# Zero regions of two cache gradients: two stored from GpSimd as two-row stores, the last one in steps of rows

## The chip, the cores and the metric

The kernel runs on one core of one Trainium2 chip. The metric is the device time in microseconds (us) of one execution; less is better. Three executions of the kernel before took 282.73, 282.97 and 284.07 us, median 282.97.

The core has five engines that run side by side and wait for each other by semaphores: PE (TensorE, matrix products and transposes), DVE (VectorE), ACT (ScalarE), POOL (GpSimd) and SP (SyncE, which here only issues DMAs). Sixteen DMA engines move data between HBM and the on-chip memory.

## The reference

One decode step of a transformer block and its gradients. With `xn` the layer-normed input, the forward part is

```
q  = xn @ wq                                # 4 batches, 32 heads of 128
k, v = k_cache[:, :, Sk-W:], v_cache[...]   # last W = 1024 of Sk = 4096 positions, 8 kv heads
p  = softmax(q k^T / sqrt(128));  o = p v
out = x + o @ wo + (gelu(xn @ w_gate) * (xn @ w_up)) @ w_down
_out, _vjp = jax.vjp(_f, A_x, A_k_cache, A_v_cache, A_wq, A_wo, B_w_gate, B_w_up, B_w_down)
_grads = _vjp(grad_out)
```

The outputs are `out` and the gradients of all eight arguments, in bf16. The gradients of `k_cache` (out_2) and `v_cache` (out_3) have the full shape (4, 8, 4096, 128). The forward part uses only the last 1024 positions, so positions 0 to 3071 of both gradients are zero, and these zeros have to be written: 2 tensors x 32 (batch, head) pairs x 3072 x 128 x 2 bytes = 50.3 MB of the 81.0 MB that the page counts as written to HBM.

## The kernel before, in words

**Stages.** First the FFN with its gradients (weights `wg`, `wu`, `wd`), then attention in four groups of two kv heads (`NT` = 4, `GP` = 2), `t` from 0 to 3. For each group the kernel transposes K and V on PE and computes scores (`kv_steps`), softmax and its gradient, `odq` (o and dq) and `fin`, and prepares four kinds of gradient pieces: `dvdk(t, 0)` for dv, `dvdk(t, 1)` for dk, and those of `dw(t)` for wo and wq. A piece is one or two matmuls into a PSUM tile, one eviction by ACT or DVE into a staging tile, and, when the staging tile is full, one store issued by SP.

**Order of the work.** Pieces are put into a queue `bg` and run one at a time by `tick` between the steps of the main work, so the last pieces of a group (dk, wo, wq) run during the next group. The program order on every engine is the order of the Python text (a manual schedule). After the last group `tick(len(bg))` at L754 empties `bg`; `zero(len(zlist))` at L755 issues the zero stores that are left. The short end (L757 to L787) computes out_0 and out_1, whose 4-row stores are issued by ACT.

**Staging tiles.** The pool `stage` has three buffers for `stg_dv` and `stg_dk`, `outp` has four for `osb_o`, `osb_q` and others. An eviction into a buffer waits until the store that used it before has landed.

**Zeros.** `ztile` (128 x 6144 bf16) holds zeros. `zlist` holds 32 zero regions; each covers two heads of one batch of one tensor, 2 x 3072 x 128 elements, and `zero(n)` (L161) stores the next n of them, one DMA of 1536 KB each, with 64 rows of 12288 bytes for each head. Calls of `zero` are spread over the program; here matter the one after each `stg_dv` and `stg_dk` store (L490, in `piece` of `dvdk`), `zero(4)` in the last group (L734) and L755. The second head's dk store of group t (`k` = 1, `g` = 1) is issued in group t + 1; the zero stores after it are issued at 120.75, 168.55 and 210.35 us for t = 0, 1, 2.

**Queues.** SP issues its DMAs in program order. Its DMAs and those of ACT take eight completion semaphores in turn, so a DMA also waits until the eighth DMA before it has landed. GpSimd issues the loads of `wo` and `wq` for the later groups (`load_w`); in the last group it has only the two `o_s` products of L463 left after its last `qmr`.

**Lines used below.** L97 and L98: evictions by ACT and DVE (`evac`). L103: the DMA in `store`, the line under which all stores appear. L279: transposes. L454 to L465: the end of `odq` for k = 0. L484: the dv and dk matmuls. L813: the end of the program.

Of the kernel before, what the change touches and what calls it, by code (L numbers as in the profile page):

```python
# [14 lines left out]
P = 128  # L15
# [3 lines left out]
def kernel(  # L19
# [28 lines left out]
    nc = tc.nc  # L48

    B, Sq, D = A_x.shape  # L50
    _, G, Sk, Dh = A_k_cache.shape
# [4 lines left out]
    K0 = Sk - W  # L56
# [4 lines left out]
    NT = G // GP  # L61
# [38 lines left out]
    def store(eng, out, in_, kind):  # L100

        eng.nop()
        d = eng.dma_start(out=out, in_=in_)  # L103
        for k in ("rest", "zeros") if kind == "rest" else ("rest",):
            tc.declare_no_dep(d.ins, group=k, reason="stores write disjoint parts of the outputs")
        tc.add_to_no_dep_group(kind, d.ins)
        return d
# [12 lines left out]
    def load_w(t, eng=nc.gpsimd):  # L120
        pool = w_pool[t % 2]
        wo_t[t] = pool.tile([P, HG, D], BF16, name="wo_sb", tag="wo")
        eng.dma_start(out=wo_t[t][:], in_=wo_v[t])
        wq_t[t] = pool.tile([P, ND, CW], BF16, name="wq_sb", tag="wq")
        eng.dma_start(out=wq_t[t][:], in_=wq_v[t])
# [30 lines left out]
    ZR = 2  # L156
    ZW = K0 * Dh * ZR // P
    ztile = const.tile([P, ZW], BF16, name="ztile")
    zlist = deque((og, b, g) for b in range(B) for g in range(0, G, ZR) for og in (out_2, out_3))

    def zero(n=1):  # L161
        for _ in range(min(n, len(zlist))):
            og, b, g = zlist.popleft()
            store(nc.sync, og[b, g:g + ZR, 0:K0, :].rearrange("g (m j) d -> m g (j d)", m=P // ZR), ztile[:], "zeros")


    nc.gpsimd.memset(ztile[:], 0.0)
# [276 lines left out]
    def odq(t, k):  # L444
        pT, blks = st[t][("PT", "dST")[k]], (v_t, k_t)[k]
        cols = pT[:].rearrange("p j (y s) -> p j s y", s=SL)
        for j in range(JB):
            q, jj = j // JQ, j % JQ
            for g in range(GP):
                nc.tensor.matmul(od_ps[g * 32:g * 32 + B * rep, k, g, :], lhsT=cols[:, jj, g * NQ + q, :],  # L450
                                 rhs=blks[(t, g)][:, j, :], start=(j == 0), stop=(j == JB - 1),
                                 tile_position=(0, g * 32))
        rows = attw.tile([P, GP, Dh], BF16, name="od_r", tag=f"od_r{k}", bufs=2)
        if k == 0:  # L454
            nc.vector.tensor_copy(out=rows[:], in_=od_ps[:, k])  # L455
        else:
            nc.scalar.activation(out=rows[:], in_=od_ps[:, k], func=ACT.Copy, scale=scale)
        st[t][("o", "dq")[k]] = rows
        if k == 0:

            o_s = attw.tile([P, GP, rep, Dh], BF16, name="o_s", tag="o_s", bufs=2)
            for g in range(GP):
                nc.gpsimd.tensor_tensor(out=o_s[:, g], in0=rows[:, g].unsqueeze(1).broadcast_to([P, rep, Dh]),  # L463
                                        in1=msk_r[:].unsqueeze(2).broadcast_to([P, rep, Dh]), op=ALU.mult)
            st[t]["os"] = o_s  # L465

    def odT(t, k):
        rows = st[t][("o", "dq")[k]]
        T_ps = transposes([rows[:, g, :] for g in range(GP)], "odT")
        rT = attw.tile([P, GP, B, rep], BF16, name="od_T", tag=f"od_T{k}")  # L470
        for g in range(GP):
            nc.vector.tensor_copy(out=rT[:, g].rearrange("p b r -> p (b r)"), in_=T_ps[:, g, g * 32:g * 32 + B * rep])
        st[t][("oT", "dqT")[k]] = rT

    def dvdk(t, k):
        src, mr, og = st[t][("P", "dS")[k]], st[t][("do", "q")[k]], (out_3, out_2)[k]
        nm = ("dv", "dk")[k]

        def piece(g, j, held):
            if j == 0:  # L480
                held["stg"] = stage.tile([P, JB, Dh], BF16, name="stg_" + nm, tag="stg")
            stg = held["stg"]
            mps = ps_w.tile([P, NQ, Dh], FP32, name="kv_ps", tag="w")
            nc.tensor.matmul(mps[:].rearrange("p q d -> p (q d)"), lhsT=src[:, j * P:(j + 1) * P],  # L484
                             rhs=mr[:, g].rearrange("p q d -> p (q d)"), start=True, stop=True)
            evac(stg[:].rearrange("p (q j) d -> p j q d", q=NQ)[:, j], mps[:], 512)
            if j == JQ - 1:
                store(nc.sync, og[:, t * GP + g, K0:Sk, :].rearrange("b (m j) d -> m b (j d)", j=JB),
                      stg[:].rearrange("p j d -> p (j d)"), "rest")
                zero()  # L490

        made = []
        for g in range(GP):
            held = {}
            made.append([lambda g=g, j=j, held=held: piece(g, j, held) for j in range(JQ)])
        return made
# [183 lines left out]
    for f4 in range(NF4):  # L680
        held = {}
        n = min(4, NF - 4 * f4)
# [34 lines left out]
    with tc.tile_pool(name="kv_b", bufs=GP, reuse_waits="tile") as kv_b, \  # L717
            tc.tile_pool(name="w_b", bufs=1, reuse_waits="tile") as w_b, \
            tc.tile_pool(name="stage", bufs=3, reuse_waits="tile") as stage:
        kv_pool[1], w_pool[1] = kv_b, w_b  # L720
        zero()
        pre(0)
        load_w(1)
        load_kv(1, 0)
        for t in range(NT):
            kv_steps(t, 0, 0)
            if t == 0:
                zero()
                load_kv(1, 1)
                zero()  # L730
            softmax(t)
            kv_steps(t, 1, 1)
            if t == NT - 1:
                zero(4)  # L734
            link(len(chain))
            softmax_d(t)
            link()
            odq(t, 0)
            load_kv(t + 2, 1)
            if t + 1 < NT:  # L740
                pre(t + 1)
            link(len(chain))
            odT(t, 0)
            odq(t, 1)
            load_kv(t + 2, 0)
            tick(2)
            odT(t, 1)
            fin(t)
            if t + 2 < NT:
                load_w(t + 2)  # L750
            (k0, k1), (o0, o1, q0, q1) = dvdk(t, 1), dw(t)
            for p in (k0, o0, k1, o1, q0, q1):
                bg.extend(p)
        tick(len(bg))  # L754
        zero(len(zlist))  # L755

        fin_ps = []  # L757
        for o in range(2):
            f_ps = ps_w.tile([B, ND, P], FP32, name="f_ps", tag="w")
            for c in range(ND):  # L760
                nc.tensor.transpose(f_ps[:, c, :], acc[:, o, c, :], ident_f[:])
            fin_ps.append(f_ps)
        acc_o = fin_ps[0][:].rearrange("b c p -> b (c p)")
        acc_d = attw.tile([B, P, ND], FP32, name="acc_d", tag="P_s")
        nc.vector.tensor_copy(out=acc_d[:].rearrange("b p c -> b c p"), in_=fin_ps[1][:])
        acc_d = acc_d[:].rearrange("b p c -> b (p c)")
        out_b = attw.tile([B, D], BF16, name="out_b", tag="pT")
        nc.vector.tensor_tensor(out=out_b[:], in0=acc_o, in1=x4[:], op=ALU.add)
        nc.scalar.dma_start(out=out_0.rearrange("b s d -> (b s) d"), in_=out_b[:])

        s1 = attw.tile([B, 1], FP32, name="s1", tag="m")
        nc.vector.reduce_sum(out=s1[:], in_=acc_d, axis=AX.X)
        pr = attw.tile([B, D], FP32, name="pr", tag="dS_s")
        s2 = attw.tile([B, 1], FP32, name="s2", tag="es")
        nc.vector.tensor_tensor_reduce(out=pr[:], in0=acc_d, in1=xn_f[:], scale=1.0, scalar=0.0,
                                       op0=ALU.mult, op1=ALU.add, accum_out=s2[:])
        nm1 = attw.tile([B, 1], FP32, name="nm1", tag="rr")
        nc.vector.tensor_scalar(out=nm1[:], in0=s1[:], scalar1=-1.0 / D, scalar2=None, op0=ALU.mult)
        nm2 = attw.tile([B, 1], FP32, name="nm2", tag="gs")
        nc.vector.tensor_scalar(out=nm2[:], in0=s2[:], scalar1=-1.0 / D, scalar2=None, op0=ALU.mult)  # L780
        nc.vector.scalar_tensor_tensor(out=pr[:], in0=xn_f[:], scalar=nm2[:, 0:1], in1=acc_d,
                                       op0=ALU.mult, op1=ALU.add)
        nc.vector.tensor_scalar(out=pr[:], in0=pr[:], scalar1=nm1[:, 0:1], scalar2=rstd[:, 0:1],
                                op0=ALU.add, op1=ALU.mult)
        dx_b = attw.tile([B, D], BF16, name="dx_b", tag="E_f")
        nc.vector.tensor_tensor(out=dx_b[:], in0=pr[:], in1=dy4[:], op=ALU.add)
        nc.scalar.dma_start(out=out_1.rearrange("b s d -> (b s) d"), in_=dx_b[:])  # L787
# [30 lines left out]
```

## Time and profile before

| what | value |
|---|---|
| median of 3 executions | 282.97 us |
| the profiled execution's own time | 283.0 us |
| its span, first to last instruction | 281.0 us |
| PE / DVE / ACT / POOL busy | 72% / 58% / 42% / 14% of the span |
| moved by DMA | 112.12 MB, mean 399 GB/s |
| share of the SP and ACT DMA queues q1 / q10 | 89.6% / 1.9% of 16 engines' span |
| share of GpSimd's DMA queue q0 | 5.6% |
| zero stores: number, size, median time from issue to landing | 32, 1536 KB, 18.1 us |

How to read it: an engine's share is its busy time over the span. The prediction shows two rows of the page's table of 40 slices, in which each digit is the busy share of one slice of 7 us in tenths. It also shows rows of a table by stages: `start:end`, length in us, then busy us and number of instructions of PE, PE's weight loads, DVE, ACT and POOL, then PE's granted clock as a share of full speed, the share of the 16 DMA engines in use, and GB/s. In the rows of waits the columns are: who waited, for what, total us, number of times, longest us. In a timeline row the columns are start, duration in us, engine, line, operation, output and input, and in brackets how long the engine had stood idle before it and what ended that.

### The profile page before, as it was taken

The numbers are of one execution on the slowest core, as the hardware profiler recorded it, in microseconds if no ns is written. First come the engines' busy times: TensorE is split into PE (matmuls) and PEld (weight loads), VectorE is DVE, ScalarE is ACT, GpSimd is POOL, SyncE is SP. The second block draws the span as 40 slices with busy tenths as digits, with TensorE's granted clock in tenths as the row PEclk, the third lists the DMA queues.
The fourth block names the chain that finished last, engine by engine and source line by source line (L and its number), as shares of the span: only waits on it lengthen the run. The fifth ranks groups of instructions, "written<-read, shape, count | busy, mean of one in ns | idle before, by whom it ended". The sixth has DMA issues, their size and how long they took to land.

```text
span 281.0 us, 6867 instructions
## 1 busy us (share of the span) xinstructions
PE 203.1 (72%) x2972; PEld 138.8 (49%) x2972; DVE 164.1 (58%) x313; ACT 117.8 (42%) x219; POOL 40.1 (14%) x40
## 2 busy tenths in 40 slices
PE   0276699959789889998999299898999599390000
PEld 0265476735456665566775156677556484140000
DVE  7946646645776655577666067767677728386000
ACT  2030386635035418764448056443866038370000
POOL 8600000007002150002250000223000400000000
PEclk9999589986999999999999969999999979977555
DMA  7999999999999999999999999999999999999990
GB/s 264 393 375 431 431 426 417 425 419 424 369 395 424 422 420 420 426 415 422 419 417 411 412 424 423 431 383 398 385 368 415 387 432 410 425 429 422 398 422 30
DMA packets 19565, 112.12 MB, mean 399 GB/s; under 512 B 1664, under 2 KB 4496, under 8 KB 11088
## 3 DMA queue, kind: packets, MB, share of 16 engines
q1 hardware_dynamic: 17744, 103.56, 89.6%
q0 software_dynamic: 1632, 6.29, 5.6%
q10 hardware_dynamic: 160, 1.84, 1.9%
q8 instruction: 23, 0.38, 0.5%
q14 instruction: 6, 0.05, 0.0%
HBM read 30.68 MB, written 81.01 MB: 397 GB/s over the span
## 4 chain that ended last, share of the span: by engine, by line
PE 47%; DMA 22%; DVE 16%; ACT 4%; issue 2%; SPq 0%; DVEq 0%; ACTq 0%
DMA out_dram<-stg_dv 13%; PE T_ps L279 8%; PE kv_ps L484 7%; DMA wd_sb<-in_B_w_down_dram 6%; PE S_ps L345 5%; PE od_ps L450 5%; DMA out_dram<-osb_g 4%; DVE T_sb L98 3%; DVE dS_s L367 2%; PE wdT_ps L279 2%; PE dwq_ps L520 2%; PE acc_ps L256 2%; PE dwd_ps L660 2%; DVE P_s L367 2%; PE wgT_ps L279 2%
## 5 line engine op out<-in xcount | busy, mean ns | idle before, releaser
L98 DVE COPY T_sb<-T_ps 128x1024 bf16<-128x1024 bf16 x64 | 44.1, 688 | 26.7 <-PE T_ps L279 26.5
L97 ACT CAST stg_dk<-kv_ps 128x512 bf16<-128x512 f32 x52 | 29.2, 588 | 31.2 <-PE kv_ps L484 12.4
L97 ACT CAST stg_dv<-kv_ps 128x512 bf16<-128x512 f32 x51 | 28.1, 588 | 24.9 <-PE kv_ps L484 24.3
L484 PE MATMUL kv_ps<-qmr,dS_s 128*128 128x512 bf16 x64 | 23.9, 414 | 11.3 <-ACT stg_dk L97 10.6
L463 POOL TENSOR_TENSOR o_s<-od_r,msk_r 128x512 bf16<-128x512 bf16 x8 | 9.1, 1157 | 110.2 <-DVE od_r L455 80.9
L484 PE MATMUL kv_ps<-domr,P_s 128*128 128x512 bf16 x64 | 21.3, 382 | 0.0
L279 PE MATMUL T_ps<-ident,vb 128*128 128x128 bf16 x256 | 20.3, 225 | 0.4 <-DVE T_sb L98 0.4
L279 PE MATMUL T_ps<-ident,kb 128*128 128x128 bf16 x256 | 20.4, 225 | 0.0
L279 PEld LDWEIGHTS <-kb 128*128 128x128 bf16 x256 | 17.5, 101 | 4.5 <-issue 1.3
L279 PEld LDWEIGHTS <-vb 128*128 128x128 bf16 x256 | 17.2, 101 | 5.0 <-issue 3.2
L97 ACT CAST osb_q<-dwq_ps 128x512 bf16<-128x512 f32 x25 | 14.6, 587 | 8.3 <-PE dwq_ps L520 7.4
L329 POOL TENSOR_TENSOR domr<-r,msk 128x1024 bf16<-128x1024 bf16 x4 | 7.6, 1892 | 71.2 <-DVE r L326 65.1
L97 ACT CAST osb_g<-dwg_ps 128x512 bf16<-128x512 f32 (+1 forms) x25 | 12.3, 544 | 12.3 <-PE dwg_ps L673 6.3
L97 ACT CAST osb_o<-dwo_ps 128x512 bf16<-128x512 f32 x24 | 13.9, 586 | 4.5 <-PE dwo_ps L505 2.9
L98 DVE CAST stg_dk<-kv_ps 128x512 bf16<-128x512 f32 x12 | 8.0, 688 | 12.0 <-DMA out_dram<-stg_dv 11.2
L98 DVE COPY wgT<-wgT_ps 128x1024 bf16<-128x1024 bf16 x14 | 9.6, 686 | 6.8 <-PE wgT_ps L279 6.8
L345 PE MATMUL S_ps<-T_sb,qm 128*32 128x256 bf16 x128 | 12.7, 387 | 0.6 <-DVE T_sb L98 0.5
L345 PE MATMUL S_ps<-T_sb,dom 128*32 128x256 bf16 x128 | 12.7, 388 | 0.1
L505 PE MATMUL dwo_ps<-dyr,o_s 128*128 128x512 bf16 x32 | 12.4, 413 | 0.3 <-ACT stg_dk L97 0.2
L98 DVE COPY woT<-woT_ps 128x1024 bf16<-128x1024 bf16 x16 | 11.0, 686 | 2.7 <-PE woT_ps L279 2.3
L484 PEld LDWEIGHTS <-dS_s 128*128 128x128 bf16 x64 | 6.2, 101 | 12.2 <-issue 11.1
L520 PE MATMUL dwq_ps<-od_r,xnm 128*128 128x256 bf16 x64 | 11.6, 274 | 0.3 <-ACT osb_q L97 0.2
(188 smaller groups left out, 385.0 us busy)
## 6 DMA issues: line engine op xcount, KB each, us to landing
out_dram<-ztile SPq DMA_DIRECT2D x32, 1536.0 KB, 18.1
kb<-in_A_k_cache_dram SPq DMA_DIRECT2D x8, 1024.0 KB, 17.4
vb<-in_A_v_cache_dram SPq DMA_DIRECT2D x8, 1024.0 KB, 20.7
out_dram<-stg_dv SPq DMA_DIRECT2D x8, 1024.0 KB, 13.0
out_dram<-stg_dk SPq DMA_DIRECT2D x8, 1024.0 KB, 20.8
out_dram<-osb_o SPq DMA_DIRECT2D x8, 512.0 KB, 17.4
out_dram<-osb_q SPq DMA_DIRECT2D x8, 512.0 KB, 13.8
out_dram<-osb_g SPq DMA_DIRECT2D x8, 448.0 KB, 14.3
```

The source lines that it names most:

```text
L97: return nc.scalar.copy(out=out, in_=in_)
L98: return nc.vector.tensor_copy(out=out, in_=in_)
L256: nc.tensor.matmul(ps[:, c, :], lhsT=lf(c), rhs=rhs, start=(k == 0), stop=(k == len(terms) - 1))
L279: nc.tensor.transpose(ps[:, i, :], a, ident[:])
L329: nc.gpsimd.tensor_tensor(out=mr[:].rearrange("p g q d -> p (g q) d"), in0=r4[:, k, :].unsqueeze(1).broadcast_to([P, SL, Dh]), in1=msk[:]. ...
L345: nc.tensor.matmul(ps[b * RB:(b + 1) * RB, :], lhsT=zt[:, b * GP + g, c0:c0 + RB], rhs=T_sb[:].rearrange("p (x b) -> p b x", b=B)[:, b, :] ...
L367: nc.vector.scalar_tensor_tensor(out=out[:], in0=src[:].unsqueeze(2).broadcast_to([P, WQ, B]), scalar=rr[:, 0:1], in1=mskb[:].unsqueeze(1) ...
L450: nc.tensor.matmul(od_ps[g * 32:g * 32 + B * rep, k, g, :], lhsT=cols[:, jj, g * NQ + q, :], rhs=blks[(t, g)][:, j, :], start=(j == 0), st ...
L463: nc.gpsimd.tensor_tensor(out=o_s[:, g], in0=rows[:, g].unsqueeze(1).broadcast_to([P, rep, Dh]), in1=msk_r[:].unsqueeze(2).broadcast_to([P ...
L484: nc.tensor.matmul(mps[:].rearrange("p q d -> p (q d)"), lhsT=src[:, j * P:(j + 1) * P], rhs=mr[:, g].rearrange("p q d -> p (q d)"), start ...
L505: nc.tensor.matmul(mps[:], lhsT=o_s[:, g].rearrange("p r d -> p (r d)")[:, i:rep * Dh:rep], rhs=dyr[:], start=True, stop=True)
L520: nc.tensor.matmul(mps[:, i].rearrange("p g d -> p (g d)"), lhsT=xnm[:, i2 * 2 + i, c * P:(c + 1) * P], rhs=dq_r[:].rearrange("p g d -> p ...
```

## The change

Three edits.

1. In `piece` of `dvdk`, the zero store after the second head's dk store is left out in groups 0, 1 and 2 (`zero(cond)` with a false condition stores none). Three regions stay in `zlist` longer.
2. In the last group, after GpSimd's two `o_s` products, `zero_pairs()` is called twice. Each call takes one region from `zlist` and stores it from GpSimd by eight DMAs. Each DMA covers two rows, one in each head of the region: seven have 16 x 3456 elements a row (source: one partition of `ztile` read 16 times), the third has 6144 elements a row.
3. At the end `zero(len(zlist))` becomes `zero(len(zlist) - 2)`, one full region, followed by `zero_steps()`. This stores the first head of a region as 64 rows of 6144 elements, 2560 positions of the second head as 64 rows of 5120, and the other 512 positions as stores of 15, 14, ... 8 and 8, 7, ... 1 rows of 512 elements. Between the two runs of small stores it stores the last full region.

SP issues 15 more DMAs than before (20 at the end in place of 2, and 3 fewer in the groups), GpSimd 16 more. The instructions of PE, DVE and ACT, and their order, are the same. The bytes written are the same.

```diff
+    def zero_pairs():
+        og, b, g = zlist.popleft()
+        zr = og[b, g:g + ZR, 0:K0, :].rearrange("g m d -> g (m d)")
+        w = 27 * Dh
+        r0 = 0
+        for i in range(8):
+            n = 16 * w if i != 2 else K0 * Dh - 7 * 16 * w
+            src = ztile[8 * i:8 * i + 8].rearrange("(a x) w -> a x w", a=2)[:, 0, :]
+            if i != 2:
+                src = src[:, 0:w].unsqueeze(1).broadcast_to([2, 16, w])
+                dst = zr[:, r0:r0 + n].rearrange("g (r w) -> g r w", r=16)
+            else:
+                src = src[:, 0:n]
+                dst = zr[:, r0:r0 + n]
+            store(nc.gpsimd, dst, src, "zeros")
+            r0 += n
+
+    def zero_steps():
+        og, b, g = zlist.popleft()
+        store(nc.sync, og[b, g, 0:K0, :].rearrange("(m j) d -> m (j d)", m=P // ZR), ztile[0:P // ZR], "zeros")
+        store(nc.sync, og[b, g + 1, 512:K0, :].rearrange("(m j) d -> m (j d)", m=64), ztile[0:64, 0:40 * Dh], "zeros")
+        r = 0
+        for n in (*range(15, 7, -1), *range(8, 0, -1)):
+            if n == 8 and r == 92:
+                zero()
+            store(nc.sync, og[b, g + 1, r * 4:(r + n) * 4, :].rearrange("(m j) d -> m (j d)", m=n), ztile[0:n, 0:4 * Dh],
+                  "zeros")
+            r += n
...
             st[t]["os"] = o_s
+            if t == NT - 1:
+                zero_pairs()
+                zero_pairs()
...
                       stg[:].rearrange("p j d -> p (j d)"), "rest")
-                zero()
+                zero(t == NT - 1 or k == 0 or g == 0)
...
         tick(len(bg))
-        zero(len(zlist))
+        zero(len(zlist) - 2)
+        zero_steps()
+        assert not zlist
```

## The prediction

> **What bounds the kernel now.** I read the table of slices first: the DMA row stands at 9 nearly everywhere, while PE falls to nothing some 15 us before the end. Then the table by stages, the DMA queue's own waits in two stretches, the timeline around the one long stall of the compute engines, and the issues with their times to landing. For single packets I used the trace's DMA records (start, length and bytes of each packet), whose numbers are given in the text.
>
> ```profile
> PE   0276699959789889998999299898999599390000
> DMA  7999999999999999999999999999999999999990
> ...
> 162.00:186.00 24.00, 22.13 (x308) 15.17 (x307) 17.66 (x32) 12.14 (x24) 2.03 (x2) 0.89 1.01 423
> 186.00:222.00 36.00, 33.47 (x494) 22.00 (x493) 24.34 (x52) 19.78 (x38) 4.51 (x3) 1.00 0.95 386
> ...
> 222.00:263.00 41.00, 23.23 (x236) 13.57 (x236) 23.16 (x42) 15.56 (x29) 2.25 (x2) 0.83 1.01 421
> 263.00:274.00 11.00, 0.00 (x0) 0.00 (x0) 0.00 (x0) 0.00 (x0) 0.00 (x0) 0.50 1.01 415
> 274.00:281.00 7.00, 0.00 (x0) 0.00 (x0) 0.00 (x0) 0.00 (x0) 0.00 (x0) 0.50 0.07 30
> ```
>
> [...] Three things are to be seen. From 222 to 274 us the engines are full (1.01; over 1 where packets of two queues overlap): this part ends by bytes alone. From 186 to 222 the share is 0.95, so about 0.06 x 36 = 2.2 us of every engine are empty. From 274 to the end only 0.07 is used: 0.07 x 16 x 7 = 8 engine-us, in effect one engine. The packet records say it exactly: twelve engines send their last byte at 274.1 to 274.2 us, three more up to 1.0 later (275.2), and one, called the late engine here, at 279.6.
>
> Why the engines are empty in 186 to 222, and what holds compute before:
>
> ```profile
> SPq L103 <- DVE stg_dv L98: 7.5, 1, 7.5
> SPq L103 <- DVE stg_dk L98: 5.5, 1, 5.5
> SPq L103 <- DVE osb_o L98: 2.9, 1, 2.9
> SPq L103 <- DVE osb_q L98: 2.3, 1, 2.3
> SPq L103 <- ACT osb_q L97: 2.2, 1, 2.2
> SPq L103 <- ACT osb_o L97: 0.5, 1, 0.5
> ...
> 161.41 0.69 DVE L98 CAST stg_dk<-kv_ps 128x512 bf16<-128x512 f32 x1 [6.48 <-DMA out_dram<-stg_dv]
> 161.42 1.07 ACT L97 CAST stg_dk<-kv_ps 128x512 bf16<-128x512 f32 x2 [7.04 <-DMA out_dram<-stg_dv]
> ...
> 162.05 0.58 PE L484 MATMUL kv_ps<-qmr,dS_s 128*128 128x512 bf16 x1 [6.00 <-ACT stg_dk L97]
> ```
>
> The first block is what SP waited for from 205 to 225 us: evictions only, never a landing. The loads of K and V are over (the last was issued at 146), so in this stretch the stores depend on compute, PE is busy 33.47 of 36 us, and the only thing that can fill the DMA queue between two results is a zero store. The second block is the opposite state: at 161.4 ACT, DVE and PE had stood 6 to 7 us until the `stg_dv` store issued at 137.8 landed, 23.5 us later. There the DMA backlog sets the pace.
>
> [...] `out_b`'s 1024-byte packets pass in the midst of the zero stores' packets.
>
> **The change, part by part.** One zero region is 1536 KB, on each engine 8 packets of 12288 bytes, 460 to 467 ns each: 3.7 us. All bytes stay; only their place changes, so what counts is whether an engine is empty where a region was, and who waits where it goes.
>
> 1. *Region after the second `dk` store in group 0 (issued 120.75).* It stands in the backlog that the compute engines wait for at 161.4. Without it that `stg_dv` lands 3.7 us sooner, the PE stall of 6.0 shrinks to 2.3, and all compute after it comes 3.7 sooner: -3.7. Bounds: 0, if another wait (the 0.7 us one for an earlier `stg_dv` at 151.8, or a load) takes its place; -6.0, if the stall goes entirely. I take -3.7.
>
> 2. *Regions of groups 1 and 2 (168.55 and 210.35).* They lie just ahead of and inside the stretch where compute sets the pace. Nothing fills their place: 2 x 3.7 = 7.4 us more empty time on each engine that runs dry before 222, which the twelve early ones do (in 186 to 222 the records show as few as 4 engines active). Nor does compute gain, since it waits for no DMA between 162 and 240.
>
> 3. *All three come back after about 217 us:* 3 x 3.7 = 11.1 us of work in a stretch that is already full.
>
> 4. *Two of them by GpSimd,* after its last two `o_s` products (they end at 224.3 before, 220.6 now; nothing is queued behind the stores on GpSimd). Seven stores give 16 x 6912 = 110.6 KB to each engine of a pair, the third 12.3 KB, against 98.3 KB in an even region. [...] The price of issuing from GpSimd isn't in this trace; the stores have until 280 us, so 0, at most 2 us if mixing two queues slows both (69 to 81 us, with GpSimd's loads under way, ran at about 380 GB/s instead of 425).
>
> 5. *The last region in steps, and SP's eight semaphores.* SP's DMAs take eight completion semaphores in turn; each waits until the eighth before it has landed. Before, the two last full regions are issued at 263 with 11 us of backlog, so the wait is hidden. Now the order at the end is full region, 64 x 6144, 64 x 5120, 15 to 8 rows, full region, 8 to 1 rows. The 8-row store waits for the landing of 64 x 5120, the full region behind it in SP's order waits too, and the engines hold only row stores of 1 KB (0.05 us a packet). Cost: landing seen 0.4 us after the last byte (records), the small issue 0.35 (the 4-row loads took 0.27 to 0.39), and 1.25 from the issue to the first packet (the `stg_dk` store issued at 209.76 found engines empty and started at 211.0): 2.0 us. The last 1-row store waits for the full region: 0.4 + 1.0 (the first x load: issue 0.8, packet at 1.8) + 0.05 = 1.45 us at the end. Bounds for the two together: 1.5 to 4.5. The steps' unevenness, at most 16 KB or 0.7 us between engines, is within that.
>
> **Sum, in us from the span's start.** Early engines end at 274.1; - 3.7 + 11.1 + 0.9 = 282.4. The three somewhat late engines add their 1.0 (most of it arose after 220, each step beside a 16 KB packet of the instruction queue, so step 2 doesn't erase it): 283.4. Waits of step 5: + 2.0 + 1.45 = 286.9. Last byte to landing 0.4 and landing to the end of the span 1.0, both as before: 288.3. The profiled execution took 283.0 for a span of 281.0, so add 2.0: 290.3, called 290. That execution is equal to the median of 282.97 within 0.03. The forecast is +7 us, 2.5% slower. Compute isn't the new end: it stopped at 258 and may be late by 15.
>
> **Rivals.**
> - *The late engine decides (faster).* For it: it alone holds the end from 275.2 to 279.6. Suppose that the queues do not run dry more than before, and that the last waits of SP are covered. Then the early engines end at 274.1 + 0.9 = 275.0, the three at 276.0, and the relieved late one at 279.6 - 6.5 = 273.1; end 276.0 + 1.4 + 2.0 = 279.4. It decides as long as the extra empty time stays below 283.0 - 279.4 = 3.6 us, or 0.1 with step 5 at full price. Against it: SP's waits of 205 to 225 have no landing in them, and step 2 alone gives 7.4.
> - *Stores of two rows all on the same two engines.* Then each gets 2 x (7 x 110.6 + 12.3) = 1573 KB, 59 us, against 7.4 + 0.9: 290 + 51 = about 341. [...]
> - *The stall at 161 goes entirely, and the tail waits cost 1.5:* 290.3 - 2.3 - 2.0 = 286. For it: the landing there was that of the late engine, 7 us behind the median engine's, so its timing can shift by more than one region.
> - *Nothing moves:* extra empty time, relief and waits cancel, 283.
>
> **How the numbers follow.** Forecast 0.72 (own range 287 to 293), small version 0.10 (286), late engine 0.07 (279.4), cancel 0.06 (283), two engines 0.05 (341). The measurement tells a change from none at about 0.5% (1.4 us). The range takes the forecast and the small version with the bounds of steps 1, 4 and 5: 285 to 294. Faster 0.07, same 0.06, slower 0.87.
>
> **What would show it.** Right: the `stg_dk` stall near 161 shrinks to about 2 to 3 us and later PE work lies some 4 us earlier; the DMA share between 182 and 218 falls from 0.95 to about 0.75 to 0.8; no lone engine at the end; a gap of about 2 us in DMA before the last full region, which is issued only when 64 x 5120 has landed. Wrong: a DMA share near 0.95 there and an end near 275 (the first rival), or two engines busy far beyond 290 (the second). If the stall stays at 6 to 7, step 1 was wrong and the time is nearer 294.

## The result, and the profile after

| kernel | median | lowest to highest | profiled span | mean PE clock |
|---|---|---|---|---|
| before | 283.39 us | 282.73 to 284.07 | 281.0 us | 0.901 |
| after | 305.74 us | 304.92 to 306.29 | 304.6 us | 0.862 |

The ratio is 1.079, with a 95% interval from 1.075 to 1.082. The change makes the kernel 22.4 us slower. The prediction had said 290, with 294 as the upper end of its range: the direction was right, two thirds of the size were missing. The mean PE clock is lower after, but the long stages at the end, where it reads 0.50, have no matrix products, so nothing waits for it there. Of the executions in the experiments, four lay over 1.5% above the fastest of their kernel and are left out of its median: 290.4 and 291.2 us of e9, 301.4 of e11 and 300.8 of e15.

The page of the kernel after, in slices of 7.6 us (the digits are tenths of a slice, the last row GB/s):

```profile
span 304.6 us, 6889 instructions
...
PE   0385798867898899989999989999696080000000
...
DMA  7999999999999999999999999895999999999735
GB/s 280 384 397 423 431 422 423 417 426 381 386 427 420 423 422 422 422 411 420 423 405 428 421 373 398 372 373 207 405 397 322 329 369 401 404 293 179 178 97 215
```

PE ends in slice 33, at 251 us (before: slice 36 of 7.0 us, 253 us), and then some 50 us follow in which DMA is nearly all that runs. What matters is the difference between the last two rows. In slices 31 to 37 the DMA row still shows 9, but the rate is 322 at their start and 179 at their end. Engines counted as busy move less than half of the 420 or so that slices 13 to 17 show. The table by stages of the same kernel says it with more precision (the columns are those of the tables by stage shown before):

```profile
176.00:216.00 40.00, 36.41 (x551) 24.47 (x553) 28.25 (x56) 21.13 (x40) 5.43 (x4) 1.00 0.86 348
227.00:240.00 13.00, 6.62 (x45) 2.56 (x42) 5.62 (x10) 5.45 (x10) 0.00 (x0) 0.90 1.00 321
240.00:256.00 16.00, 6.78 (x32) 3.25 (x31) 11.33 (x20) 5.57 (x10) 1.71 (x3) 0.71 1.01 377
256.00:268.00 12.00, 0.00 (x0) 0.00 (x0) 0.00 (x0) 0.00 (x0) 1.19 (x2) 0.50 1.03 409
268.00:285.00 17.00, 0.00 (x0) 0.00 (x0) 0.00 (x0) 0.00 (x0) 1.76 (x3) 0.50 1.00 212
285.00:296.00 11.00, 0.00 (x0) 0.00 (x0) 0.00 (x0) 0.00 (x0) 0.00 (x0) 0.50 0.53 130
296.00:302.00 6.00, 0.00 (x0) 0.00 (x0) 0.00 (x0) 0.00 (x0) 0.00 (x0) 0.50 0.71 277
```

There are three kinds of loss. In the first row the share is 0.86: engines without work (e2 below shows that the regions missing there are why). From 227 to 240 and from 268 to 285 the share is 1.00 at 321 and 212 GB/s: engines with work that is slow. From 285 to 296 the share is 0.53: some engines are done while others still work. The prediction had the first kind, and only 3.5 us of the last.

GpSimd's own timeline at the end (the columns are those of a timeline row shown before):

```profile
217.28 4.70 POOL L103 DMA_DIRECT2D out_dram<-ztile  x8
240.09 0.59 POOL L103 DMA_DIRECT2D out_dram<-ztile  x1 [18.12 <-DMA out_dram<-ztile]
248.49 0.59 POOL L103 DMA_DIRECT2D out_dram<-ztile  x1 [7.81 <-DMA out_dram<-ztile]
...
275.98 0.59 POOL L103 DMA_DIRECT2D out_dram<-ztile  x1 [1.01 <-DMA out_dram<-ztile]
```

The eight stores of the first region go out at once. Each store of the second waits until one of the first eight has landed (the first 18.12 us, all eight together 49.9), so the last is issued only at 276. By the packet records these stores are under way until 297.8 us. And what SP waits for from 262 us on (total us, times, longest):

```profile
SPq L103 <- DMA out_dram<-ztile: 14.8, 6, 5.3
```

### The profile page after: what moved, and what is told of

Same layout as the page of the kernel before. It is cut to its first block, busy times and chain, and to the rows that moved or that the text cites. A ratio compares the mean times of both kernels' runs of the same rounds, so it can differ in the third digit from the quotient of the medians.

```text
span 304.6 us, 6889 instructions
## 1 busy us (share of the span) xinstructions
PE 202.0 (66%) x2962; PEld 138.5 (45%) x2972; DVE 164.0 (54%) x313; ACT 118.0 (39%) x219; POOL 49.5 (16%) x56
## 4 chain that ended last, share of the span: by engine, by line
PE 39%; DMA 30%; DVE 11%; ACT 4%; POOL 2%; issue 2%; another core or an unknown queue 1%; SPq 0%; POOLq 0%; DVEq 0%; ACTq 0%
DMA out_dram<-ztile 16%; PE T_ps L310 8%; PE kv_ps L518 6%; PE S_ps L376 5%; DMA wd_sb<-in_B_w_down_dram 5%; PE od_ps L481 4%; DMA out_dram<-osb_g 4%; DMA out_dram<-osb_d 3%; DMA out_dram<-osb_o 2%; DVE T_sb L98 2%; PE acc_ps L287 2%; DVE wqT L98 2%; PE wdT_ps L310 2%; DVE P_s L398 2%; PE dwq_ps L554 2%
## 5 line engine op out<-in xcount | busy, mean ns | idle before, releaser
L518 PE MATMUL kv_ps<-qmr,dS_s 128*128 128x512 bf16 x62 | 22.4, 397 | 10.5 <-ACT stg_dk L97 9.8
L518 PE MATMUL kv_ps<-domr,P_s 128*128 128x512 bf16 x58 | 19.9, 387 | 0.1
L103 POOL DMA_DIRECT2D out_dram<-ztile x16 | 9.4, 589 | 49.9 <-DMA out_dram<-ztile 49.9
L97 ACT CAST osb_g<-dwg_ps 128x512 bf16<-128x512 f32 (+1 forms) x25 | 12.3, 544 | 10.6 <-DMA out_dram<-osb_g 4.7
L376 PE MATMUL S_ps<-T_sb,qm 128*32 128x256 bf16 x128 | 12.7, 386 | 0.6 <-DVE T_sb L98 0.5
```

Of the source, the lines that this page charges most:

```text
L97: return nc.scalar.copy(out=out, in_=in_)
L376: nc.tensor.matmul(ps[b * RB:(b + 1) * RB, :], lhsT=zt[:, b * GP + g, c0:c0 + RB], rhs=T_sb[:].rearrange("p (x b) -> p b x", b=B)[:, b, :] ...
```

## Experiments 1 to 5: the parts alone

**e1_pairs_only**: before, with the two regions stored by GpSimd and nothing deferred or cut into steps.

```diff
             st[t]["os"] = o_s
+            if t == NT - 1:
+                zero_pairs()
+                zero_pairs()
```

> Only the GpSimd part: the kernel before with its last two zero regions stored by GpSimd in two-row stores in the last group; no region is deferred out of groups 0 to 2, no steps at the end. Theory A (the prediction: two-row stores cost only their bytes, and deferral and the waits at the end make the loss): 279 to 284 us. Theory B (the loss is the two-row stores: each also puts some 16 packets of 4 bytes on each of the other 14 engines, which take turns with SP's packets, slow the engines and make GpSimd's stores land late): 293 to 303 us.

**e2_defer_only**: the deferral alone; the three regions come back as full ones from SP at the end.

```diff
-                zero()
+                zero(t == NT - 1 or k == 0 or g == 0)
```

> Only the deferral: the three zero regions after the dk stores of groups 0 to 2 are stored at the end by SP as full regions; no GpSimd stores, no steps. Theory A as in the prediction (compute comes 3.7 us earlier): 274.1 - 3.7 + 11.1 + 1.0 + 1.4 + 2.0 = 286 us. Theory B, with compute 6.9 us earlier as the changed kernel's trace shows (its four regions in the last group are issued at 212.8 instead of 219.7): 283 us, no change.

**e3_steps_only**: the last two regions as in the change, the rest as before.

```diff
-        zero(len(zlist))
+        zero(len(zlist) - 2)
+        zero_steps()
```

> Only the steps at the end: the kernel before with its last region stored as 64 x 6144, 64 x 5120 and stores of 15 to 1 rows, the last full region between the small ones. Both theories put the same price on the waits of SP (2.0 before the full region, 1.45 at the end): the late engine lands the 64 x 5120 store at 275.9, + 2.0 + 3.7 + 1.45 + 1.4 + 2.0 = 286.5 us. If the waits are covered after all: 283.

**e4_no_pairs**: e2 and e3 together, that is, the whole change without GpSimd's stores.

> The whole change without the GpSimd stores: deferral and steps, the two regions stored by SP as full regions before the steps. Theory A: 289 us, and nearly the changed kernel's time if the GpSimd stores are harmless. Theory B: 283 + 3.45 = 286 us, so that the GpSimd stores account for nearly 20 us of the changed kernel's loss.

**e5_pool_full**: as e1, but GpSimd stores the two regions as ordinary ones, 128 rows each; `zero` takes the issuing engine as an argument here.

```diff
-    def zero(n=1):
+    def zero(n=1, eng=nc.sync):
...
-            store(nc.sync, ...
+            store(eng, ...
...
+            if t == NT - 1:
+                zero(2, nc.gpsimd)
```

> As e1_pairs_only, but GpSimd stores the same two regions, at the same place, as two ordinary full regions (128 rows of 6144) in place of sixteen two-row stores. If GpSimd's queue itself is what costs: about 297 us as in e1. If the two-row form is (either through the 4-byte packets or through the rows read): 283 us, at most 285.

| kernel | median us | ratio to before, 95% |
|---|---|---|
| e1_pairs_only | 296.76 | 1.051 (1.043 to 1.059) |
| e2_defer_only | 283.13 | 1.000 (0.998 to 1.002) |
| e3_steps_only | 287.35 | 1.015 (1.011 to 1.019) |
| e4_no_pairs | 290.37 | 1.025 (1.018 to 1.031) |
| e5_pool_full | 283.46 | 1.001 (1.000 to 1.002) |

GpSimd's stores cost 13.5 us alone and 15.4 on top of the rest (305.74 - 290.37). Deferral costs nothing by itself, the steps some 4 alone and 7.2 once deferral is there. (The four executions of e4 lie in two pairs, near 289 and near 292, so figures that rest on e4 are uncertain by some 2 us.) And it isn't that GpSimd issues them: with full regions (e5) the same engine, the same queue and the same bytes cost nothing that can be measured. It is the form of the stores.

The table by stages shows why deferral is neutral. The first row is that of the kernel before, the other two are e2's:

```profile
176.00:222.00 46.00, 42.35 (x675) 28.94 (x673) 32.15 (x65) 23.95 (x45) 6.54 (x5) 1.00 0.96 393
...
176.00:222.00 46.00, 41.35 (x622) 28.53 (x623) 29.11 (x59) 21.51 (x41) 6.76 (x4) 0.93 0.89 362
274.00:281.00 7.00, 0.00 (x0) 0.00 (x0) 0.00 (x0) 0.00 (x0) 0.00 (x0) 0.50 0.56 237
```

The engines do run dry in the middle (0.89 of 46 us in use, in place of 0.96), and in the last 7 us they have work that they had not before (0.56 in place of 0.07). By the DMA records 13 engines now end at 277.8 to 278.1 us, 3.8 later than before, while the late engine ends at 279.4 (before 279.6). Deferral moved work into time that the late engine held anyway. Compute comes earlier, too. SP's issue of the four zero stores of the last group shows it, in the kernel before, in e2 and in the kernel after:

```profile
219.74 4.40 SPq L103 DMA_DIRECT2D out_dram<-ztile  x4
...
212.43 4.21 SPq L103 DMA_DIRECT2D out_dram<-ztile  x4
...
212.82 4.19 SPq L103 DMA_DIRECT2D out_dram<-ztile  x4
```

## Experiments 6 to 10: which property of the two-row stores

The records of single packets gave the first hint. In e1 GpSimd's 6912-byte packets take 321 ns on average, a quarter of them over 330, where the same bytes at a full region's pace need 262 (12288 bytes in 460 to 467). The candidates were the number of packets (theory B1 below) and the rows of `ztile` that they read (B2). Of packets of 4 bytes GpSimd's queue has 3420 more than before. An estimate from the counts: before, its six loads have 96, 16 each; if each of the 16 two-row stores has these 16 too, and besides, on each of the 14 engines that it doesn't use, as many as it has data packets in a row (16, in the third store 1), that makes 14 x 14 x 16 + 2 x 14 + 16 x 16 = 3420.

**e6_pairs_r9**: e1 with fewer and longer packets.

```diff
-        w = 27 * Dh
+        w = 48 * Dh
...
-            n = 16 * w if i != 2 else K0 * Dh - 7 * 16 * w
+            n = 9 * w if i != 2 else K0 * Dh - 7 * 9 * w
```

> As e1_pairs_only with the same bytes for each engine in fewer packets: rows of 9 x 6144 instead of 16 x 3456, so that each of the large stores puts 9 packets of 4 bytes on the other engines instead of 16. Theory B1 (packets of 4 bytes that take turns with SP's packets): the loss of 13.5 shrinks about as 9 to 16, to 7.6: 291 us. Theory B2 [...]: the bytes and rows read are the same: 297 us.

**e7_pairs_rows**: e1 with other source rows in the last four stores of a region.

```diff
-            src = ztile[8 * i:8 * i + 8].rearrange("(a x) w -> a x w", a=2)[:, 0, :]
+            p0 = 8 * i if i < 4 else 32 + 8 * i
+            src = ztile[p0:p0 + 8].rearrange("(a x) w -> a x w", a=2)[:, 0, :]
```

> As e1_pairs_only, only the source rows of the last four pairs changed: rows 64 to 92 instead of 32 to 60 of ztile[...]. Theory B2 [...]: most of the loss goes, 283 to 287 us. Theory B1 (4-byte packets): nothing changes, 297 us.

**e9_rows_and_r9**: both edits together.

> Both edits of e6 and e7 together: source rows 64 to 92 for the last four pairs and rows of 9 x 6144. Theory: what is left of e7's loss (7.2 us) is that GpSimd's packets take turns with SP's on every engine, some 242 of them against 156 of SP's after 225 us, so that the second round of GpSimd's stores is issued late (to 279 us) and lands after SP's queue has ended. With 9 + 1 packets a store there are 160, about as many as SP has: 280 to 284 us. Rival: the rest is the two-row form in another way (its eight semaphores, one engine pair for each store): 288 to 290 us as in e7.

**e10_one_region**: e9 with one region from GpSimd in place of two.

> As e9, but only one region goes to GpSimd; the other is the last full region of SP as before. No store of GpSimd waits for an earlier one. If the third pair of engines holds the late one, that engine sends 86 KB less (3.2 us) and ends at 276.4 instead of 279.6, the others at 274.6 to 275.7: 279.5 to 280 us, faster than the kernel before. If it doesn't: 283.5 us.

e6 took 298.19 us (ratio 1.053, 1.050 to 1.056): fewer packets alone bring nothing. e7 took 290.39 (1.025, 1.021 to 1.029): the same packets of the same size from other rows bring back 6.4 us. So rows matter. e9 took 286.0 and 286.5 us, a miss against its 280 to 284, and 4 us below e7; two executions are too few to say that the longer packets help once rows are better. e10 took 284.57 (1.006, 1.004 to 1.008). In it two engines end at 280.8 and 281.0, some 4 us behind the rest (275.6 to 277.3), so that the end is set by single engines as before, and the relief that it hoped for isn't there. A part of the loss remained in both kernels, and in e9 a third of GpSimd's packets were still slow (over 1.25 times the full pace). The guess was that other rows would do better still.

What the runs show is an effect of rows. In the change the eight stores of a region read rows between 0 and 60 of `ztile`, two rows each, all in its first 64 partitions. In e7 the last four read rows 64 to 92 in place of 32 to 60, and that was the only difference. Why it matters was not shown: the packet records name no engine. The rows of e7, and later of e16, were chosen on an assumption that no run tests by itself: that certain rows, read at the same time, slow each other.

## Experiments 13, 14, 16, 17: the small third store

**e13_even_pairs**: as e9, but eight equal stores and no small one (the lines that these replace are left out).

```diff
+        w = 48 * Dh
+        n = 8 * w
+        for i in range(8):
+            p0 = 8 * i if i < 4 else 32 + 8 * i
+            src = ztile[p0:p0 + 8].rearrange("(a x) w -> a x w", a=2)[:, 0, :].unsqueeze(1).broadcast_to([2, 8, w])
+            dst = zr[:, i * n:(i + 1) * n].rearrange("g (r w) -> g r w", r=8)
+            store(nc.gpsimd, dst, src, "zeros")
```

> The kernel before with the two regions from GpSimd alone, as in e9 (rows 0 to 28 and 64 to 92 of ztile), but all eight stores equal: two rows of 8 x 6144 elements, one in each head, 1 MiB apart. If the unequal third pair and its longer neighbours cost e9 its 3 to 5 us, it takes 283 to 284 us. If two rows at a distance of 1 MiB, or stores of two rows as such, are the cause, it stays at 286 to 290.

**e14_pairs_one_head**: the same, with the two rows of a store in one head.

```diff
-            dst = zr[:, i * n:(i + 1) * n].rearrange("g (r w) -> g r w", r=8)
+            dst = og[b, g + i // 4, 768 * (i % 4):768 * (i % 4 + 1), :].rearrange("(a r m) d -> a r (m d)", a=2, r=8)
```

> As e13, but the two rows of a store lie one after the other in one head (96 KB apart in place of 1 MiB); four stores for each head. The number of stores, their rows, packets and source are those of e13. If the distance of 1 MiB costs the rate, 283 to 284 us and a DMA rate above 400 GB/s between 228 and 268 us. If stores of two rows as such are the cause, the same time as e13 within 1 us.

e13 took 283.83 us and e14 284.09, both with the ratio 1.003 (1.002 to 1.004). Two-row stores as such cost 0.3%, and whether the two rows lie 1 MiB or 96 KB apart in the output makes no difference that these runs show. What e9 has in addition is the small third store (and, with it, shares of nine packets in place of eight). The guess was that the rows that suit a store depend on the large stores ahead of it and not on the small one. e16 therefore gives the large stores their rows in one round: they start at row 0, 8, 16, 24, 64, 72, 80, 88, each store takes the next, the small store takes none (it reads rows 0 and 4), and the second region goes on where the first ended. If that was wrong, 290 us or more was expected, as in e7.

**e16_rows_follow**: e1, with the source rows of each large store chosen in that round, and nothing else changed. The 16 x 3456 elements, the small store and the uneven shares stay.

```diff
-            src = ztile[8 * i:8 * i + 8].rearrange("(a x) w -> a x w", a=2)[:, 0, :]
+            e = 2 * zcur[0] % 16 if i != 2 else 0
+            zcur[0] += i != 2
+            p0 = 4 * (e % 8) + 64 * (e // 8)
+            src = ztile[p0:p0 + 8].rearrange("(a x) w -> a x w", a=2)[:, 0, :]
```

> As e1 (the kernel before with the two regions from GpSimd alone, 16 x 3456 elements a row, a small third store), but with other source rows: [...] e1's 13.5 us shrink to the 0.9 of the uneven shares and at most 2 for the small packets: 283 to 286 us, q0 packets of 6912 bytes at about 265 to 290 ns. [...] the rows are wrong for most stores and it takes 290 or more, as e7 did.

**e17_after_rows**: the whole changed kernel with this edit alone. What it can take back is what GpSimd's stores cost on top of e4 (290.37 us).

> The whole changed kernel with the rows of e16 and nothing else changed. [...] they now cost 1 to 3 us: 291 to 293.5. If uneven shares and small packets cost by themselves when SP waits for landings at the end, it stays above 297.

| kernel | median us | ratio to before, 95% | GpSimd's data packets: bytes, mean ns | over 1.25 times the full pace |
|---|---|---|---|---|
| e1 | 296.76 | 1.051 (1.043 to 1.059) | 6912, 321 | 25% |
| e7 | 290.39 | 1.025 (1.021 to 1.029) | 6912, 312 | 23% |
| e16 | 286.12 | 1.010 (1.009 to 1.012) | 6912, 270 | 3% |
| after | 305.74 | 1.079 (1.075 to 1.082) | 6912, 354 | 31% |
| e17 | 296.12 | 1.046 (1.044 to 1.048) | 6912, 281 | 7% |
| e9 | 286.27 (two executions) | not given | 12288, 585 | 34% |
| e13 | 283.83 | 1.003 (1.002 to 1.004) | 12288, 478 | 3% |

The same stores, with the same sizes, in the same order, are 10.6 us cheaper alone (e1 to e16) and 9.6 us cheaper in the whole (after to e17), by the choice of the rows that they read. The table by stages of e1 and then of e16 shows it where GpSimd's packets are under way:

```profile
227.00:240.00 13.00, 12.31 (x156) 7.50 (x152) 8.69 (x17) 9.14 (x18) 2.09 (x4) 0.95 1.00 362
240.00:256.00 16.00, 6.71 (x24) 2.94 (x24) 5.58 (x9) 5.08 (x10) 1.17 (x2) 0.68 1.00 354
...
275.00:282.00 7.00, 0.00 (x0) 0.00 (x0) 0.00 (x0) 0.00 (x0) 1.14 (x2) 0.50 0.52 169
282.00:289.00 7.00, 0.00 (x0) 0.00 (x0) 0.00 (x0) 0.00 (x0) 0.59 (x1) 0.50 0.45 143
```

```profile
227.00:240.00 13.00, 12.50 (x148) 7.28 (x145) 8.56 (x17) 9.04 (x18) 2.35 (x5) 0.91 1.00 381
240.00:256.00 16.00, 9.24 (x38) 4.50 (x37) 8.71 (x14) 6.72 (x12) 2.09 (x4) 0.79 1.02 415
...
275.00:282.00 7.00, 0.00 (x0) 0.00 (x0) 0.00 (x0) 0.00 (x0) 0.59 (x1) 0.50 0.47 176
282.00:285.00 3.00, 0.00 (x0) 0.00 (x0) 0.00 (x0) 0.00 (x0) 0.00 (x0) 0.50 0.00 0
```

The engines are in use throughout in both from 240 to 256 (1.00 and 1.02), but e1 moves 354 GB/s and e16 415. In e1 the bytes that were not moved then are moved after 282. Both e7 and e16 read rows 0 to 28 and 64 to 92, and only which store reads which of them differs: e16's round leaves 3% slow packets, e7's order 23%. Why was not shown; the records name no engine.

e16, just above what was expected, still costs 2.9 us, 2.1 above e13's 0.8. It has the uneven shares, more packets, and a second region that is issued late (its last store at 275.3 us, against 261.2 in e13). Which of these it is was not separated. e17 stays 2.6 us above the upper end of what was expected; the 64-row stores, to which the next section comes, may have a part in it.

## Experiments 8, 11, 15, 18: the steps, and everything mended

**e8_steps_128**: e4 with the two large stores of the steps as 128 rows of half the length.

```diff
-        ... "(m j) d -> m (j d)", m=P // ZR), ztile[0:P // ZR], "zeros")
-        ... "(m j) d -> m (j d)", m=64), ztile[0:64, 0:40 * Dh], "zeros")
+        ... "(m j) d -> m (j d)", m=P), ztile[:, 0:24 * Dh], "zeros")
+        ... "(m j) d -> m (j d)", m=P), ztile[:, 0:20 * Dh], "zeros")
```

> As e4_no_pairs, but the two large stores of the steps have 128 rows of half the length (128 x 3072 and 128 x 2560) instead of 64 rows, the same bytes. In the trace of e3 two engines took 0.79 to 0.82 us for 10240 bytes of the 64-row store that others moved in 0.385. If 64 rows halve the engines' rate, 3.4 us of e4's 7.1 go: 287 us. If not: 290 us.

It took 287.00 us (1.013, 1.009 to 1.018), 3.4 less than e4's 290.37. (The executions of e4 and e8 don't overlap, but they spread over 3.6 and 2.5 us.) In e4 the 10240-byte packets take 808 ns on average, in e8 5120-byte packets take 208: 12.7 against 24.6 bytes per ns. The 64-row stores read partitions 0 to 63 alone, as the two-row stores of the change do, and the 128-row stores read all 128; why that should matter was not shown. That these packets are not slow by their size shows in e3: the first engine that comes to the 64 x 5120 store takes 385 ns for each of its four packets; then, with the others at it, most take 750 to 800, about twice as much; and at its end one engine again takes 385, while two others, at the same time, still take 790 to 815. The stages of e4 and then of e8:

```profile
268.00:275.00 7.00, 0.00 (x0) 0.00 (x0) 0.00 (x0) 0.00 (x0) 0.00 (x0) 0.50 1.03 305
275.00:282.00 7.00, 0.00 (x0) 0.00 (x0) 0.00 (x0) 0.00 (x0) 0.00 (x0) 0.50 0.65 184
```

```profile
268.00:275.00 7.00, 0.00 (x0) 0.00 (x0) 0.00 (x0) 0.00 (x0) 0.00 (x0) 0.50 0.93 364
275.00:282.00 7.00, 0.00 (x0) 0.00 (x0) 0.00 (x0) 0.00 (x0) 0.00 (x0) 0.50 0.58 234
```

**e11_mended**: the whole changed kernel with the edits of e7, e6 and e8.

> The whole changed kernel with three mends and nothing else: the last four GpSimd pairs read rows 64 to 92 of ztile in place of 32 to 60; the large GpSimd stores have 9 x 6144 elements a row in place of 16 x 3456; the two large stores of the steps have 128 rows in place of 64. The DMAs, their number and their order stay. [...] the three mends bring back what they brought back apart: the steps with 128 rows took 287.0 us without GpSimd's stores, and the mended GpSimd stores alone cost 0 to 5 us. So about 289 us (287.5 to 292), some 16 of the 22 us. If the loss comes from having two queues side by side at the end, whatever their rows and packets, it stays above 297.

Its three executions took 293.4 to 297.5 us, median 294.59 (1.041, 1.036 to 1.046), not 289. The parts didn't add up.

**e15_full_first**: e11 with the last full region ahead of all small stores.

```diff
+        zero()
         r = 0
         for n in (*range(15, 7, -1), *range(8, 0, -1)):
-            if n == 8 and r == 92:
-                zero()
```

> As e11, but in the steps the last full region is issued ahead of all small row stores and not between the two runs of them; nothing else changes. If e11's time above its parts comes from the wait ahead of that region (between 280 and 286 us three to six engines were busy, the region moved from 286 to 289), the engines that are done early take the region meanwhile: about 291.5 us (290 to 293), 4 to 5 less than e11, and no stretch in which all engines stand still before the last region. If the loss is of rate and not of waits, 295 to 297.

It took 294.49 us (1.039, 1.034 to 1.043): 0.1 less, where 4 to 5 were expected. The wait ahead of that region was not what e11 lacked. The stages of e15 say where to look, since the share is full and the rate isn't:

```profile
256.00:275.00 19.00, 0.00 (x0) 0.00 (x0) 0.00 (x0) 0.00 (x0) 0.88 (x2) 0.50 1.01 352
275.00:282.00 7.00, 0.00 (x0) 0.00 (x0) 0.00 (x0) 0.00 (x0) 0.00 (x0) 0.50 1.02 423
```

**e18_all_mended**: e15 with the rows of e16.

> e15 with the rows of e16 in place of its own (rows 9 x 6144, large steps of 128 rows, last full region ahead of the small rows). On the same reasons: e8's 287.0 us with up to 2 less for the region moved ahead and 1 to 2 more for GpSimd's stores: 286 to 288.5. If the interaction seen in e11 and e15 has another cause than rows, above 292.

It took 289.75 us (1.023, 1.022 to 1.025), 4.7 less than e15, though 1.3 above what was expected. Slow packets of GpSimd fell from 34% to 1%. So of the 22.4 us the changed kernel loses, 16.0 come back without moving a byte to another place in the output or to another engine that issues it; the order changes in one place (the last full region).

## Experiment 12: a version faster than both

If the late engine sets the end, the cheapest relief is a region of which it gets less. The plan assumes that a 4-row store by SP falls on four engines of which it is none. And of the three deferred regions only group 0's lies where compute waits for DMA; the two others lie where the DMA queue is short of work.

**e12_four_rows**: before, with that one region deferred, and one of its heads stored by four rows.

```diff
+    def zero_four():
+        og, b, g = zlist.popleft()
+        src = ztile[0:16].rearrange("(a x) w -> a x w", x=4)[:, 0, :].unsqueeze(1).broadcast_to([4, 16, ZW])
+        store(nc.sync, og[b, g, 0:K0, :].rearrange("(a r j) d -> a r (j d)", a=4, r=16), src, "zeros")
+        store(nc.sync, og[b, g + 1, 0:K0, :].rearrange("(m j) d -> m (j d)", m=P), ztile[:, 0:24 * Dh], "zeros")
...
-                zero()
+                zero(t != 0 or k == 0 or g == 0)
...
         tick(len(bg))
+        zero_four()
         zero(len(zlist))
```

> The kernel before, with the region after the second dk store of group 0 alone left for the end, and there stored first, one head as a store of 4 rows (4 x 16 x 6144 elements, rows 0, 4, 8 and 12 of ztile), the other head as 128 rows of 3072. The four rows should fall on four engines of which the late one is none[...]; every other engine then carries 98.3 KB / 2 = 49 KB less of this region, 1.85 us. If the lone late engine sets the end of the kernel before: it ends at 279.6 - 1.85 = 277.75 us, the four loaded ones at 270.9 (early end less one region's 3.2 us of moved work) + 5.5 + 1 at most, so the kernel takes 281.2 us, 0.7% less than before. If the late engine's lateness comes back by other work beside it, or one of the four loaded engines becomes the last: 283 or above.

It took 280.98 us (0.992, 0.990 to 0.993), 2.4 us less than before. Its stages:

```profile
176.00:222.00 46.00, 41.47 (x647) 28.61 (x648) 29.68 (x61) 22.05 (x43) 6.76 (x4) 0.96 1.00 414
...
263.00:274.00 11.00, 0.00 (x0) 0.00 (x0) 0.00 (x0) 0.00 (x0) 0.00 (x0) 0.50 0.74 312
274.00:281.00 7.00, 0.00 (x0) 0.00 (x0) 0.00 (x0) 0.00 (x0) 0.00 (x0) 0.50 0.12 49
```

From 176 to 222 us no engine runs dry (1.00, against 0.89 in e2). By the records eleven engines end at 269.3 to 271.5, the four that took the rows at 276.6, and the late one at 277.6 (expected 277.75; before 279.6). So the path is the one that was expected, by the times at which the engines end; the deferral and the four rows were not tried apart.

## Why the prediction was wrong, step by step

- **Step 4 failed.** "The price of issuing from GpSimd isn't in this trace; the stores have until 280 us, so 0, at most 2 us ..." It was 15.4 us on top of the rest (13.5 alone). Nor did the time until 280 us suffice: in the kernel after these stores end at 297.8. The sum counted bytes per engine at 26.7 bytes per ns (12288 in 460 ns) and never asked which rows the stores read. Of the 15.4, 9.6 are the rows (e17); why rows matter was not shown. The other 5.8 are not separated in the whole. Alone, 2.9 us remain with the rows of e16, for 0.9 of which the sum had a term, the uneven shares; with the steps mended too, about as much remains, 2.8 (e18 against e8, between which the last full region moves as well). The bound was taken from loads by GpSimd (256 packets of 4096 bytes each in before), not from two-row stores; for e5's full regions, 0.1% slower than before, it held. The rival with all these stores on the same two engines fell: by the records of the kernel after up to ten of GpSimd's 6912-byte packets are under way at once. The 0.9 in the sum and the relief of 6.5 us in the first rival were estimates that assume the sixteen stores to go round the engines in turn, which no run shows, and e10 found no such relief.
- **Step 1 was mis-sized.** The stall near 161 us was to shrink to 2.3 us and give 3.7. It went entirely (from 137 to 166 us neither e2 nor the kernel after has a wait for a `stg_dv` store left): `zero(4)` is issued at 212.8 us after and 219.7 before, so compute is 6.9 us earlier, more than the bound of 6.0.
- **Steps 2 and 3 were right in kind.** The regions that are missing leave engines empty, and they come back at the end. The sign, a smaller DMA share from 182 to 218 us, is there, though 0.86 in place of the 0.75 to 0.8 that was named. With step 1 at its true size the early engines should end 11.1 - 6.9 = 4.2 us later; in e2 they end 3.8 later. The late engine's lateness was nearly erased by the empty time (1.5 us behind most others in e2, 5.5 before), so a relief of it would have bought little.
- **Step 5 had the waits right and missed the pace of the 64-row stores.** In e3 the gap ahead of the last full region is there: the last byte of the 64 x 5120 store at 276.9, the region's first packet at 278.9, 2.0 us as worked out. That the 64-row stores themselves run at half pace (12.7 bytes per ns in e4, 24.6 for 128 rows in e8) was in no term: 3.4 us (e8 against e4, uncertain as said).
- **Two errors cancelled in e4.** The sum without step 4's 0.9 is 289.4 and e4 took 290.4, though step 1 was 3.2 us too small a gain and the half pace was missing. The forecast looked good where it was wrong twice.
- **The faster rival fell** by its own criterion: the extra empty time in e2 was 3.8 us, just above its 3.6 (0.1 with step 5 at full price), and it had no term for the rows either.

The sum of the parts, as measured: 0 for deferral, 7.2 for the steps (3.4 of them the 64 rows), 15.4 for GpSimd's stores (9.6 of them the rows). The last two are not independent. The 10240-byte packets of the 64-row stores, 808 ns on average in e4, take 1281 in the kernel after and 855 in e17: with the change's rows GpSimd's stores slow the 64-row stores further than with those of e16. How many us this makes was not measured.

## What to carry to other kernels

The choice of the on-chip rows that the stores read was worth some 10 us here by itself (10.6 from e1 to e16, 9.6 from after to e17), with bytes, packet sizes, order and issuing engine unchanged. Before you reshape a store, look at the rows that it reads as well as at its bytes, and try others. In a profile the sign was a DMA share of 1.00 at a falling GB/s (212 from 268 to 285 us in the kernel after, where some 420 stood before): then look at the time of single packets, not at queues and waits. And ask of each region of idle-time work whether it stands in a stretch that waits for DMA or in one that is short of DMA work: moving one region from the first and two from the second came to nothing here (e2), moving only the one from the first, in e12, went with a gain.

## What was not expected of the hardware

- 64-row stores from partitions 0 to 63 ran at half the pace of 128-row ones: 10240 bytes in 808 ns against 5120 in 208; in e3 single engines took 385 ns for such a packet, others 790 at the same time.
- A two-row store by GpSimd comes with many 4-byte packets: 3420 more for the 16 stores of after, 2048 in e13 (14 x 8 + 16 = 128 a store, as the estimate above gives). They were cheap here: e13 costs 0.8 us in all.
- Which of rows 0 to 28 and 64 to 92 each store by GpSimd reads made 4.3 us: 290.39 us in e7 with 23% slow packets, 286.12 in e16 with 3%. Why was not shown.
- GpSimd's ninth store waits for one of the eight before it to land, as SP's does (up to 5.3 us from 262 us on in the kernel after): there it waited 18.1 us, and the second region was issued over 36 us (240.1 to 276.6).
- One engine is 4 to 5 us behind the others at the end in before (279.6 against at most 275.2) and in e13 (280.4 against at most 276.4). Why it is late was not tried.
